# A two-branch mixer on one core: 64x64 fold tiles, more identity transposes, w1 loaded in whole rows, and three tiles' work ahead of the q fold

## The chip, the cores and the metric

The kernel runs on one NeuronCore of a Trainium2 chip. The metric is the time of one execution on the device in microseconds; before the change it was 660.29 us, the median of three runs (658.58 to 660.71). Five engines work side by side, each through its own list of instructions in order: PE (matrix multiplication, with its weight loads shown as PEld), DVE (vectors), ACT (activations), POOL and SP. SP and POOL, and ACT for one kind, also issue transfers (DMA).

## The reference

x is 2048 x 512. It is normalised, and then two branches are added to it: a linear attention with 32 heads of 16, whose feature map is a learned 16 x 16 matrix per head and two softmaxes, and a gated MLP whose gate mixes the rows.

```python
xn = _layernorm(x, axis=-1)
return x + _A_ref(xn, A_wqkv, A_w_phi, A_wo) + _B_ref(xn, B_w_in, B_w_sp, B_b_sp, B_w_out)
...
pq = jnp.einsum("bhsd,hdf->bhsf", q, w_phi)
pk = jnp.einsum("bhsd,hdf->bhsf", k, w_phi)
phi_k = jnp.concatenate([_softmax(pk, axis=-1), _softmax(-pk, axis=-1)], axis=-1)
kv = jnp.einsum("bhsf,bhsd->bhfd", phi_k, v)
z = jnp.einsum("bhsf->bhf", phi_k)
...
z = _gelu(jnp.einsum("bsd,df->bsf", x, w_in))
z2 = _layernorm(z[..., Fh:], axis=-1)
g = jnp.einsum("ts,bsf->btf", w_sp, z2) + b_sp[None, :, None]
return jnp.einsum("bsf,fd->bsd", z1 * g, w_out)
```

## The kernel before

x is taken in 16 tiles of 128 rows. To keep the precision of float32 with faster matmuls, every operand is held as two parts: h, the value rounded by ACT (`round_h`), and l, the rest, which DVE subtracts (`rest_l`). A product is then three matmuls, h by h, h by l and l by h (`mm3`, L49 to L53), so every product leaves rows with L51, L52 and L53.

The first phase, which this change touches, makes for each tile s: the centred x, its transpose xT by four PE transposes (L261), v (`proj_v`, 12 matmuls of 512 columns), k and q with their features (`proj_k`, `proj_q`; `softmax_pair` has DVE find maximum and minimum, subtract, ACT take the exponential, DVE sum and invert), the sum kv of k's features by v (`add_kv`, tile kvps, L291), and the first half z1 of the MLP's projection (`z1_raw`, tile zps, 24 matmuls of 344 columns), which ACT copies out of PSUM and sends to memory. Later phases make z2, the row mix (tile g, 30% of the chain of work that ended last) and the output; they are not touched.

The weights of q and k are not used as they come. The matrices of the heads are first multiplied into them: `fold(i, ...)` does it for k (i = 1) and q (i = 0) from the transposed weights wrow and the block-diagonal matrix bd. It is 128 small float32 matmuls, each of which leaves two PE and two PEld records in the trace; each contracts over 64 rows, writes 32 partitions and streams 64 columns, so that eight fit side by side in the array. `folded` then splits the four PSUM tiles into h and l: four ACT roundings and four DVE differences.

The order at the beginning is written by hand. `queue` is a stack of orders: each instruction given to `keep` must be issued, on its engine, before everything that is recorded later, until `queue.close()`. Behind that, a scheduler orders each engine's list. `warm_up(12)` puts 12 transposes of the identity on PE ahead of the first real work. Before the loop over tiles stand: tile 0 and 1 transposed, v(0), the k fold, v(1), k(0) with the transposes of tile 2 in its middle, the q fold. In the loop, tile s does k(s), then centres and transposes tile s + 2, then kv(s), v(s + 2) and its share of z1.

SP issues the loads in order: x of tiles 0 and 1, the four parts of wv, bd, the k weights, x of tile 2, the q weights, x of tile 3, the bias. w1, the weights of z1, comes in the loop at s = 1, in eight pieces of 128 x 344, through the five x slots (`load_win` with tag "x"), so these loads wait for x slots to be given back and later x tiles wait for them. Each piece is split by ACT and DVE on its own.

PSUM has eight banks. Those of za are taken in turn by the first half of a fold and by z1.

Of the kernel before, what the change touches and what calls it, by code (L numbers as in the profile page):

```python
# [10 lines left out]
F32 = mybir.dt.float32  # L11
# [18 lines left out]
XB = 5  # L30
# [5 lines left out]
def mixer(ctx: ExitStack, tc: tile.TileContext, x, x_t, wv, wqkT, phi_bd, wo, w_in, wst, b_r, w_out, out):  # L36
# [4 lines left out]
    def round_h(eng, h, src):  # L41
        if eng is act:
            return act.activation(h, src, AF.Copy).ins  # L43
        return eng.tensor_copy(h, src).ins
# [4 lines left out]
    def mm3(dst, a, b, start, stop):  # L49
        (ah, al), (bh, bl) = a, b  # L50
        pe.matmul(dst, ah, bh, start=start, stop=False)  # L51
        pe.matmul(dst, ah, bl, start=False, stop=False)  # L52
        return pe.matmul(dst, al, bh, start=False, stop=stop).ins  # L53
# [27 lines left out]
    def rstd_of(mv, r, stats=None):  # L81
        if stats is not None:
            dve.bn_aggr(mv, stats)
        pool.tensor_scalar_add(mv[:, 1:2], mv[:, 1:2], EPS_LN)
        pool.tensor_tensor(r, mv[:, 1:2], mhalf, op=ALU.pow)
# [11 lines left out]
    def bc(ap, n):  # L97
        return ap.unsqueeze(2).to_broadcast([P, n, DH])

    def softmax_pair(pl, src, tag, scale=1.0, ebufs=2):  # L100

        mm = pl.tile([P, 2, H], F32, tag=tag + "mm", bufs=1, name="mm")
        dve.tensor_reduce(mm[:, 0], heads(src), axis=AX.X, op=ALU.max)
        dve.tensor_reduce(mm[:, 1], heads(src), axis=AX.X, op=ALU.min)
        er = pl.tile([P, NF + 2 * H], F32, tag=tag + "e", bufs=ebufs, name="e")
        e, r = er[:, :NF], er[:, NF:]
        e2 = e.rearrange("p (h a d) -> p h a d", a=2, d=DH)
        dve.tensor_tensor(e2[:, :, 0], heads(src), bc(mm[:, 0], H), op=ALU.subtract)
        dve.tensor_tensor(e2[:, :, 1], bc(mm[:, 1], H), heads(src), op=ALU.subtract)  # L109
        act.activation(e, e, AF.Exp, scale=scale)  # L110
        sm = pl.tile([P, 2 * H], F32, tag=tag + "sm", bufs=1, name="sm")
        dve.tensor_reduce(sm, heads(e), axis=AX.X, op=ALU.add)  # L112
        dve.reciprocal(r, sm)
        return er
# [7 lines left out]
    def zproj(ps, s, w, order=(0, 1)):  # L122

        if ps in (za, kv_ps_p):
            p = [ps.tile([P, D], F32, tag="z", name="zps") for _ in range(2)]
        else:
            q = ps.tile([P, 2, D], F32, tag="z", name="zps")
            p = [q[:, k] for k in range(2)]
        t = xT[s]
        for k, j in enumerate(order):  # L130
            for c in range(ND):
                cs = slice(c * P, (c + 1) * P)
                mm3(p[k][:, :FC], (t[:, 0, cs], t[:, 1, cs]), (w[j][0][:, c], w[j][1][:, c]), c == 0, c == ND - 1)
        return [(slice(k, k + 1), p[k][:, :FC].unsqueeze(1)) for k in range(2)] if ps in (za, kv_ps_p) else [(slice(0, 2), q[:, :, :FC])]

    def z1_raw(pl, ps, s, bufs):
# [24 lines left out]
    with ExitStack() as p0:  # L161
# [13 lines left out]
        def stage(name, dt=F32):  # L175
            return xz.tile([P, 2, FH], dt, tag="xz", name=name)
# [15 lines left out]
        def fold(i, wT, tiles):  # L192


            for g in range(NG):
                for c in range(ND):
                    for m in range(4):
                        for r in range(2):
                            rows, cols = slice(r * HP, (r + 1) * HP), slice(m * QP, (m + 1) * QP)
                            ins = pe.matmul(tiles[c // 2][r][cols, c % 2, g], wT[g][rows, c * P + m * QP:c * P + (m + 1) * QP],  # L200
                                            bd[rows, g * P + r * HP:g * P + (r + 1) * HP], start=True, stop=True,
                                            skip_group_check=True).ins
            return ins

        def folded(i, tiles, keep=lambda **ins: None, between=lambda: None):
            for k in range(2):
                if k:
                    between()
                for r in range(2):
                    h, l = (w[:, i, 2 * k:2 * k + 2].rearrange("p c (g a b) -> p c g a b", g=NG, a=2)[:, :, :, r] for w in (wqk_h, wqk_l))  # L210
                    keep(act=round_h(act, h, tiles[k][r]))
                    keep(dve=rest_l(l, tiles[k][r], h))

        def fold_tiles(pools):
            return [[pl.tile([P, D], F32, tag=tag, name="fold").rearrange("p (c g b) -> p c g b", c=2, g=NG)
                     for _ in range(2)] for pl, tag in pools]
# [3 lines left out]
        def load_win(dst, j, stp, tag, bufs):  # L220
            for c in range(ND):
                t = stp.tile([P, D if tag == "x" else FC], F32, tag=tag, bufs=bufs, name="wst_")
                split_w(dst[0][:, c], dst[1][:, c], w_in[c * P:(c + 1) * P, j * FC:(j + 1) * FC], t[:, :FC])
# [10 lines left out]
        def fetch(s):  # L234
            if s < NT:
                xt[s] = load_x(s)

        def split_x(src):
            t = xz.tile([P, 2, FH], F32R, tag="xz", name="xT")
            xT.append(t)  # L240
            src = src.rearrange("p a b -> p (a b)")
            return round_h(act, t[:, 0, :D], src), rest_l(t[:, 1, :D], src, t[:, 0, :D])

        def stats(s, keep=lambda **ins: None):
            st6 = wk.tile([P, 6], F32, tag="st6", name="st6")
            dve.bn_stats(st6, xt[s])
            keep(dve=dve.bn_aggr(mv_x[:, s], st6).ins)

        def neg_mean(s):
            nm = wk.tile([P, 1], F32, tag="nm", name="nm")  # L250
            pool.tensor_scalar_mul(nm, mv_x[:, s, 0:1], -1.0)
            return nm

        def center(s, nm):
            return act.activation(xt[s], xt[s], AF.Identity, bias=nm).ins
# [13 lines left out]
            split_x(transposed(s)[0])  # L269

        def keep_v(s, p):
            v[s] = wk.tile([P, D], F32, tag="v", name="v")
            act.activation(v[s], p, AF.Copy, scale=r_x[:, s:s + 1])

        def proj_v(s):
            keep_v(s, proj(s, wv_h, wv_l))

        def proj_k(s):
            return softmax_pair(wk, proj(s, wqk_h[:, 1], wqk_l[:, 1]), "k", r_x[:, s:s + 1])
# [19 lines left out]
        fetch(2)  # L299
        wqT = load_rows(wqkT[:D])  # L300
        fetch(3)
        sp.dma_start(bias, b_r)


        def keep(**ins):
            for i in ins.values():
                queue.enter_context(tc.issue_after(i))

        def warm_up(n):

            t = ps.tile([P, ND, P], F32, tag="mm", name="idle")
            for k in range(n):
                i = pe.transpose(t[:, k % ND], ident, ident).ins
            keep(pe=i)
# [1 line left out]
        queue = ExitStack()  # L316
        tbl = wk.tile([P, 1], F32, tag="nm", name="tbl")
        keep(act=act.activation(tbl, mhalf, AF.Identity, bias=mhalf).ins)
        warm_up(12)
        stats(0, keep)  # L320
        keep(dve=dve.tensor_scalar(xt[0], xt[0], mv_x[:, 0, 0:1], None, op0=ALU.subtract).ins)
        stats(1, keep)
# [8 lines left out]
        def turned(s):  # L331
            pt, i = transposed(s)
            keep(pe=i)
            return pt

        def split_t(pt):
            i, j = split_x(pt)
            keep(act=i, dve=j)

        split_v(0)  # L340
        split_t(turned(0))
        for c in range(1, ND):
            split_v(c)
        keep(act=center(1, nm))
# [12 lines left out]
        keep(pe=fold(1, wkT, tiles))  # L357
        proj(1, wv_h, wv_l, p, (1, 2, 3))
        keep(pe=proj.last)
        stats(2, keep)  # L360
        nm = neg_mean(2)
        rstd_of(mv_x[:, 2], r_x[:, 2:3])
        folded(1, tiles, keep, lambda: keep(act=center(2, nm)))
        keep_v(1, p)
        kvps = kv_ps_p.tile([P, D], F32, tag="z", name="kvps")
        kv_acc = kvps[:, :NG * HP].rearrange("p (g b) -> p g b", b=HP)
        p = ps.tile([P, D], F32, tag="mm", name="proj")
        proj(0, wqk_h[:, 1], wqk_l[:, 1], p, (0, 1))
        keep(pe=proj.last)
        pt = turned(2)  # L370
        proj(0, wqk_h[:, 1], wqk_l[:, 1], p, (2, 3))
        keep(pe=proj.last)
        split_x(pt)
        ek = softmax_pair(wk, p, "k", r_x[:, 0:1])
        tiles = fold_tiles(((za, "z"), (ps, "mm")))
        keep(pe=fold(0, wqT, tiles))
        folded(0, tiles, keep)
        n1 = nq = 0
        for s in range(NT):
            fetch(s + 4)  # L380
            er = proj_k(s) if s else ek
            if 0 < s < NT - 2:
                centered(s + 2)
            while nq < (s - 2) * NT // (NT - 3):
                proj_q(nq)
                nq += 1
            add_kv(s, er)
            if s + 2 < NT:
                proj_v(s + 2)
            if s == 1:  # L390
                for j in range(2):
                    load_win(w1[j], j, wk, "x", XB)
                queue.close()
            while n1 < s * (NT - LAG) // (NT - 1):
                z1_raw(wk, za, n1, 2)
                n1 += 1

# [510 lines left out]
```

## Time and profile before

| | before |
|---|---|
| median of three runs | 660.29 us |
| the profiled execution, its own time | 660.35 us |
| its span, first to last instruction | 658.6 us |
| PE idle from 0 to 50 us, by its rows, beyond the 1.81 us at the start | 0.49, 0.69, 3.10, 1.72, 1.17, 2.46 us and smaller ones |
| PE idle from 50.2 to 215 us | none |

The profile page gives the busy time of each engine, and the span in 40 slices of 16.5 us, where a digit is a busy share in tenths. A row of the timeline gives start, length, engine, source line, operation, output and inputs, shape and count, and in brackets the idle time before it with what ended it. "issue" there means that the engine waited for nothing that the profile shows. A view by stages gives the busy time of every engine in each stretch and PEclk, the share of the full clock that was granted to PE.

### The profile page before, as it was taken

The page shows a single profiled execution, that of the slowest core. Times are in us where ns is not written, and L with a number is a line of the kernel's source. Part 1 is how long each engine was busy: PE and PEld are TensorE (multiplying, and loading weights), DVE is VectorE, ACT ScalarE, POOL GpSimd, SP SyncE. Part 2 cuts the span into 40 slices and gives each one's busy share as a digit, 9 for nine tenths or more (in the row PEclk, how much of TensorE's full clock was granted, in tenths as well). Part 3 has the DMA queues.
Part 4 walks back from the last instruction along what each step waited for, and adds up shares of the span by engine and source line. Part 5 has one row for each costly group of instructions (what it writes and reads, how often), then busy time and mean ns, then how long its engine had stood idle before and what let it go on. Part 6 is the DMA issues. An engine that isn't in the chain of part 4 may idle for free.

```text
span 658.6 us, 12104 instructions
## 1 busy us (share of the span) xinstructions
PE 642.5 (98%) x4740; PEld 577.6 (88%) x4740; DVE 509.4 (77%) x922; ACT 278.6 (42%) x463; POOL 97.0 (15%) x184
## 2 busy tenths in 40 slices
PE   7779999999999999999999999999999999999997
PEld 5658888888888999999999999999999878888885
DVE  4478798898889767999998687786787688989521
ACT  4344344343333264888544344344344332333330
POOL 4024122111101102554000100101000000000100
PEclk9789999999999999999999999999999999999999
DMA  8045436434434683000444534424448686775620
GB/s 313 15 98 142 129 104 172 131 88 133 129 102 135 191 286 124 32 1 25 133 131 133 169 113 137 161 89 169 126 146 273 199 316 245 284 252 218 237 66 32
DMA packets 39082, 98.45 MB, mean 149 GB/s; under 512 B 4881, under 2 KB 6929, under 8 KB 39025
## 3 DMA queue, kind: packets, MB, share of 16 engines
q1 hardware_dynamic: 27824, 56.78, 26.8%
q0 software_dynamic: 8896, 35.26, 17.7%
q10 hardware_dynamic: 2304, 5.64, 2.2%
q8 instruction: 37, 0.61, 0.4%
q14 instruction: 21, 0.16, 0.1%
HBM read 56.37 MB, written 26.61 MB: 126 GB/s over the span
## 4 chain that ended last, share of the span: by engine, by line
PE 94%; DMA 2%; DVE 2%; issue 1%; ACT 1%; SPq 0%; ACTq 0%
PE g L53 10%; PE g L51 10%; PE g L52 10%; PE proj L51 7%; PE proj L52 7%; PE proj L53 7%; PE zps L53 6%; PE zps L52 6%; PE zps L51 6%; PE pout L51 5%; PE pout L52 5%; PE pout L53 5%; PE po L803 1%; PE ptq L788 1%; PE kvps L291 1%; PE pout L817 1%
## 5 line engine op out<-in xcount | busy, mean ns | idle before, releaser
L51 PE MATMUL g<-B,A 128*128 128x344 f32 x448 | 143.3, 320 | 0.0
L53 PE MATMUL g<-B,A 128*128 128x344 f32 x448 | 143.3, 320 | 0.0
L52 PE MATMUL g<-B,A 128*128 128x344 f32 x448 | 143.2, 320 | 0.0
L53 PEld LDWEIGHTS g<-B,A 128*128 128x128 f32 x448 | 84.2, 188 | 0.0
L51 PEld LDWEIGHTS g<-B,A 128*128 128x128 f32 x448 | 84.2, 188 | 0.0
L52 PEld LDWEIGHTS g<-B,A 128*128 128x128 f32 x448 | 84.1, 188 | 0.0
L47 DVE TENSOR_TENSOR A<-S,A 128x512 fp32r<-128x512 f32 x64 | 43.7, 688 | 33.7 <-ACT A L43 32.9
L43 ACT ACTIVATE A<-S 128x512 fp32r<-128x512 f32 x64 | 40.0, 631 | 60.7 <-PE g L53 36.4
L110 ACT ACTIVATE e<-e,r_x 128x1024 f32<-128x1024 f32 x32 | 36.8, 1151 | 39.7 <-DVE e L109 39.2
L51 PE MATMUL proj<-wqk_h,xT 128*128 128x512 f32 x128 | 52.0, 407 | 0.0
L52 PE MATMUL proj<-wqk_l,xT 128*128 128x512 f32 x128 | 51.0, 399 | 0.0
L53 PE MATMUL proj<-wqk_h,xT 128*128 128x512 f32 x128 | 50.9, 398 | 0.0
L43 ACT ACTIVATE A<-wf 128x512 fp32r<-128x512 f32 x64 | 33.4, 522 | 36.9 <-PE g L53 33.1
L51 PE MATMUL zps<-w_0h,xT 128*128 128x344 f32 x128 | 41.6, 325 | 2.5 <-ACT w_0h L43 2.5
L112 DVE TENSOR_REDUCE sm<-e 128x64 f32<-128x1024 f32 x32 | 38.7, 1209 | 5.1 <-ACT e L110 5.0
L52 PE MATMUL zps<-w_0l,xT 128*128 128x344 f32 x128 | 41.3, 323 | 0.1
L53 PE MATMUL zps<-w_0h,xT 128*128 128x344 f32 x128 | 41.3, 322 | 0.0
L51 PE MATMUL zps<-w_1h,xT 128*128 128x344 f32 x128 | 41.2, 322 | 0.0
L53 PE MATMUL zps<-w_1h,xT 128*128 128x344 f32 x128 | 40.9, 320 | 0.0
L52 PE MATMUL zps<-w_1l,xT 128*128 128x344 f32 x128 | 40.8, 319 | 0.0
L47 DVE TENSOR_TENSOR A<-wf,A 128x512 fp32r<-128x512 f32 x64 | 35.4, 554 | 3.7 <-ACT A L43 3.3
L139 ACT ACTIVATE z1f<-zps,r_x 128x344 f32<-128x344 f32 (+1 forms) x29 | 16.4, 576 | 37.6 <-PE zps L53 32.6
(194 smaller groups left out, 1433.7 us busy)
## 6 DMA issues: line engine op xcount, KB each, us to landing
wf<-in_wst SPq DMA_DIRECT2D x64, 256.0 KB, 3.3
e_d<-e POOLq DMA_DIRECT2D x16, 544.0 KB, 4.6
et<-e_d SPq DMA_DIRECT2D x16, 544.0 KB, 5.5
zacc<-e POOLq DMA_DIRECT2D x16, 512.0 KB, 4.6
er<-et POOLq DMA_DIRECT2D x12, 512.0 KB, 4.0
u_d<-z1t POOLq DMA_DIRECT2D x16, 368.0 KB, 4.5
u<-u_d SPq DMA_DIRECT2D x15, 368.0 KB, 4.4
z_d<-z1f ACTq DMA_DIRECT2D x16, 344.0 KB, 3.6
```

The costliest lines, as they stand in the source:

```text
L43: return act.activation(h, src, AF.Copy).ins
L47: return (eng or dve).tensor_tensor(l, src, h.bitcast(F32), op=ALU.subtract).ins
L51: pe.matmul(dst, ah, bh, start=start, stop=False)
L52: pe.matmul(dst, ah, bl, start=False, stop=False)
L53: return pe.matmul(dst, al, bh, start=False, stop=stop).ins
L110: act.activation(e, e, AF.Exp, scale=scale)
L112: dve.tensor_reduce(sm, heads(e), axis=AX.X, op=ALU.add)
L139: act.activation(z[:, k], p, AF.Copy, scale=r_x[:, s:s + 1])
L291: pe.matmul(kv_acc[k:k + QP, m // 4], vs[:, m * QP:(m + 1) * QP], e[:, m * HP:(m + 1) * HP], start=s == 0 and m < 4, stop=s == NT - 1, ski ...
L788: pe.transpose(pt[:, a, k].bitcast(F32R), src, ident_r)
L803: lasts[3] = pe.matmul(po[r][c * QP:(c + 1) * QP, k], kvT[rows, m // 2, cols], fs[m // 4][rows, m // 2 % 2], start=True, stop=True).ins
L817: pe.matmul(p, rt, w, start=False, stop=False)
```

## The change

The fold takes 64 columns of weights at a time in place of 32: 64 matmuls, four side by side. `warm_up` makes 15 transposes of the identity in place of 12, and five more between the transposes of tile 0 and the first v. w1 is loaded in four whole rows of 128 x 688 behind x of tile 3, into slots that later hold xT, and is split by `split_w1` in four pieces of 128 x 688 in the middle of the softmax of k(0). Tile 3 is centred and transposed ahead of the loop. v(2), k(1) and z1(0) are issued ahead of the q fold, which moves into the loop's first pass. `v` gets a third buffer, and `queue.close()` moves from s = 1 to s = 3.

```diff
-    def softmax_pair(pl, src, tag, scale=1.0, ebufs=2):
+    def softmax_pair(pl, src, tag, scale=1.0, ebufs=2, meanwhile=lambda: None):
...
         act.activation(e, e, AF.Exp, scale=scale)
+        meanwhile()
         sm = pl.tile([P, 2 * H], F32, tag=tag + "sm", bufs=1, name="sm")
...
-                    for m in range(4):
+                    for m in range(2):
                         for r in range(2):
-                            rows, cols = slice(r * HP, (r + 1) * HP), slice(m * QP, (m + 1) * QP)
-                            ins = pe.matmul(tiles[c // 2][r][cols, c % 2, g], wT[g][rows, c * P + m * QP:c * P + (m + 1) * QP],
+                            rows, cols = slice(r * HP, (r + 1) * HP), slice(m * HP, (m + 1) * HP)
+                            ins = pe.matmul(tiles[c // 2][r][cols, c % 2, g], wT[g][rows, c * P + m * HP:c * P + (m + 1) * HP],
                                             bd[rows, g * P + r * HP:g * P + (r + 1) * HP], start=True, stop=True,
...
-            v[s] = wk.tile([P, D], F32, tag="v", name="v")
+            v[s] = wk.tile([P, D], F32, tag="v", bufs=3, name="v")
...
         fetch(3)
+        w1r = [stage("w1row") for _ in range(2)]
+        for c in range(ND):
+            sp.dma_start(w1r[c // 2][:, c % 2], w_in[c * P:(c + 1) * P, :FH])
         sp.dma_start(bias, b_r)
...
-        warm_up(12)
+        warm_up(15)
...
-        split_t(turned(0))
+        pt = turned(0)
+        warm_up(5)
+        split_t(pt)
...
+        keep(act=center(3, settled(3)))
         p = ps.tile([P, D], F32, tag="mm", name="proj")
         proj(0, wqk_h[:, 1], wqk_l[:, 1], p, (0, 1))
...
-        split_x(pt)
-        ek = softmax_pair(wk, p, "k", r_x[:, 0:1])
-        tiles = fold_tiles(((za, "z"), (ps, "mm")))
-        keep(pe=fold(0, wqT, tiles))
-        folded(0, tiles, keep)
-        n1 = nq = 0
+        split_t(pt)
+
+        def split_w1():
+            for j in range(2):
+                for k in range(2):
+                    h, l = (w[:, 2 * k:2 * k + 2] for w in w1[j])
+                    src = w1r[k][:, :, j * FC:(j + 1) * FC]
+                    keep(act=round_h(act, h, src))
+                    keep(dve=rest_l(l, src, h))
+
+        ek = [softmax_pair(wk, p, "k", r_x[:, 0:1], meanwhile=split_w1)]
+        proj_v(2)
+        keep(pe=proj.last)
+        ek.append(proj_k(1))
+        keep(pe=proj.last)
+        split_x(turned(3))
+        z1_raw(wk, za, 0, 2)
+        keep(pe=zproj.last)
+        n1, nq = 1, 0
         for s in range(NT):
             fetch(s + 4)
-            er = proj_k(s) if s else ek
-            if 0 < s < NT - 2:
+            er = ek[s] if s < len(ek) else proj_k(s)
+            if 1 < s < NT - 2:
                 centered(s + 2)
...
             add_kv(s, er)
-            if s + 2 < NT:
+            if s == 0:
+                tiles = fold_tiles(((za, "z"), (ps, "mm")))
+                keep(pe=fold(0, wqT, tiles))
+                folded(0, tiles)
+            elif s + 2 < NT:
                 proj_v(s + 2)
-            if s == 1:
-                for j in range(2):
-                    load_win(w1[j], j, wk, "x", XB)
-                queue.close()
...
+            if s == 3:
+                queue.close()
```

PE at its beginning, before, up to the first matmuls of v(0) (idle is the identity, pt the transposes of tile 0):

```order
L313 MATMUL idle<-ident 128x128 x12
L261 MATMUL pt<-ident,xt 128x128 x4
L51 MATMUL proj<-wv_h,xT 128x512
L52 MATMUL proj<-wv_l,xT 128x512
L53 MATMUL proj<-wv_h,xT 128x512
```

And after:

```order
L317 MATMUL idle<-ident 128x128 x15
L262 MATMUL pt<-ident,xt 128x128 x4
L317 MATMUL idle<-ident 128x128 x5
L51 MATMUL proj<-wv_h,xT 128x512
L52 MATMUL proj<-wv_l,xT 128x512
L53 MATMUL proj<-wv_h,xT 128x512
```

Eight transposes of the identity are added, three ahead of tile 0's and five behind them.

PE around the q fold, before: the end of k(0), the fold and the beginning of v(2).

```order
L51 MATMUL proj<-wqk_h,xT 128x512
L52 MATMUL proj<-wqk_l,xT 128x512
L53 MATMUL proj<-wqk_h,xT 128x512
L200 MATMUL fold<-bd,wrow 32x64 x128
L51 MATMUL proj<-wv_h,xT 128x512
L52 MATMUL proj<-wv_l,xT 128x512
```

After: the end of k(1), the transposes of tile 3, the ends of z1(0) and the fold with the beginning of v(3); v(2) and all of k(1) stand ahead of this piece.

```order
L52 MATMUL proj<-wqk_l,xT 128x512
L53 MATMUL proj<-wqk_h,xT 128x512
L262 MATMUL pt<-ident,xt 128x128 x4
L51 MATMUL zps<-w_0h,xT 128x344
...
L53 MATMUL zps<-w_1h,xT 128x344
L201 MATMUL fold<-bd,wrow 64x64 x64
L51 MATMUL proj<-wv_h,xT 128x512
L52 MATMUL proj<-wv_l,xT 128x512
```

The fold has half the instructions and has moved behind v(2), k(1), the transposes of tile 3 and z1(0).

ACT from the first two parts of the k fold on, before (the activations are the centring of tile 2, v(1), the rounding of xT(2) and the exponential of k(0)):

```order
L43 ACTIVATE wqk_h<-fold 128x8x64 x2
L255 ACTIVATE xt<-xt,nm 128x512
L43 ACTIVATE wqk_h<-fold 128x8x64 x2
L273 ACTIVATE v<-proj,r_x 128x512
L43 ACTIVATE xT<-pt 128x512
L110 ACTIVATE e<-e,r_x 128x1024
```

And after:

```order
L43 ACTIVATE wqk_h<-fold 128x8x64 x2
L256 ACTIVATE xt<-xt,nm 128x512
L43 ACTIVATE wqk_h<-fold 128x8x64 x2
L256 ACTIVATE xt<-xt,nm 128x512
L274 ACTIVATE v<-proj,r_x 128x512
L43 ACTIVATE xT<-pt 128x512
L43 ACTIVATE w_0h<-w1row 128x688 x2
L43 ACTIVATE w_1h<-w1row 128x688 x2
L274 ACTIVATE v<-proj,r_x 128x512
L110 ACTIVATE e<-e,r_x 128x1024
```

A second centring, that of tile 3, now stands ahead of v(1) and xT(2), and the four roundings of w1 and v(2) ahead of the exponential of k(0).

More of the change, by code (lines that the diff above doesn't have):

```diff
@@ L132, in zproj @@
                 cs = slice(c * P, (c + 1) * P)
-                mm3(p[k][:, :FC], (t[:, 0, cs], t[:, 1, cs]), (w[j][0][:, c], w[j][1][:, c]), c == 0, c == ND - 1)
+                zproj.last = mm3(p[k][:, :FC], (t[:, 0, cs], t[:, 1, cs]), (w[j][0][:, c], w[j][1][:, c]), c == 0, c == ND - 1)
         return [(slice(k, k + 1), p[k][:, :FC].unsqueeze(1)) for k in range(2)] if ps in (za, kv_ps_p) else [(slice(0, 2), q[:, :, :FC])]
@@ L359, in mixer, with settled @@
         keep(pe=proj.last)
-        stats(2, keep)
-        nm = neg_mean(2)
-        rstd_of(mv_x[:, 2], r_x[:, 2:3])
+        def settled(s):
+            stats(s, keep)
+            nm = neg_mean(s)
+            rstd_of(mv_x[:, s], r_x[:, s:s + 1])
+            return nm
+        nm = settled(2)
         folded(1, tiles, keep, lambda: keep(act=center(2, nm)))
```

## The prediction

> **What bounds the kernel now.** I read the page first, for the engine that is never free.
>
> ```profile
> PE 642.5 (98%) x4740; PEld 577.6 (88%) x4740; DVE 509.4 (77%) x922; ACT 278.6 (42%) x463; POOL 97.0 (15%) x184
> PE   7779999999999999999999999999999999999997
> PEclk9789999999999999999999999999999999999999
> q8 instruction: 37, 0.61, 0.4%
> ```
>
> PE is the bound: 98% busy, and below nine tenths only in the first three slices (49 us) and the last. So the change, which leaves PE's matrix work as it is, can gain only in those first slices, and everything it gains there must still stand when the full stretch begins. Next I cut that head into stages (columns: stage, its length, busy us of PE, PEld, DVE, ACT, POOL, granted clock, DMA share, GB/s).
>
> ```profile
> 18.44:27.30 8.86, 8.86 (x93) 6.94 (x93) 3.23 (x5) 3.95 (x7) 0.00 (x0) 0.67 0.03 8
> 27.30:29.12 1.82, 1.82 (x163) 1.65 (x163) 1.74 (x4) 0.00 (x0) 0.00 (x0) 1.00 0.23 76
> 30.84:44.80 13.96, 10.20 (x165) 8.15 (x165) 10.71 (x20) 6.17 (x13) 3.94 (x10) 1.00 0.37 78
> 44.80:48.20 3.40, 3.08 (x9) 2.15 (x8) 2.76 (x5) 3.40 (x7) 0.00 (x0) 0.50 0.39 113
> 48.20:69.08 20.88, 20.88 (x164) 17.73 (x164) 15.71 (x30) 9.53 (x15) 7.00 (x14) 1.00 0.60 155
> 69.08:215.00 145.92, 145.92 (x1029) 122.18 (x1028) 129.17 (x189) 54.13 (x68) 24.64 (x44) 1.00 0.44 123
> ```
>
> From 48.20 us PE has no idle time at full clock. Before that it loses time to idleness (3.76 us in 30.84 to 44.80) and to a halved clock (0.50 in 44.80 to 48.20, a mean of 0.67 in 18.44 to 27.30). PE's order in time shows the single losses (start, length, form, count, in brackets idle time and its releaser), and where to measure: 69.08, where v of tile 5 begins.
>
> ```profile
> 1.81 2.82 PE L313 MATMUL idle<-ident 128*128 128x128 f32 x12 [1.81 <-POOL ident masks.py:199]
> 5.12 1.11 PE L261 MATMUL pt<-ident,xt 128*128 128x128 f32 x4 [0.49 <-DVE xt L321]
> 6.92 0.79 PE L51 MATMUL proj<-wv_h,xT 128*128 128x512 f32 x1 [0.69 <-ACT xT L43]
> ...
> 13.27 2.07 PE L200 MATMUL fold<-bd,wrow 64*32 64x64 f32 x188
> 18.44 1.32 PE L200 MATMUL fold<-bd,wrow 64*32 64x64 f32 x68 [3.10 <-issue]
> ...
> 27.31 1.81 PE L200 MATMUL fold<-bd,wrow 64*32 64x64 f32 x162
> 30.84 1.17 PE L200 MATMUL fold<-bd,wrow 64*32 64x64 f32 x94 [1.72 <-issue]
> ...
> 39.66 0.66 PE L261 MATMUL pt<-ident,xt 128*128 128x128 f32 x4 [1.17 <-ACT xt L255]
> 43.57 0.42 PE L51 MATMUL zps<-w_0h,xT 128*128 128x344 f32 x1 [2.46 <-ACT w_0h L43]
> 69.08 0.40 PE L51 MATMUL proj<-wv_h,xT 128*128 128x512 f32 x1
> ```
>
> Each fold is broken by a stall named "issue": 3.10 and 1.72 us. Between the two stalls lie 93 + 163 = 256 PE and 256 PEld records, 512 instructions. The page has 37 packets on q8 for 4740 + 4740 records, about 256 a packet, and one packet fell into the first stall:
>
> ```profile
> q8 instruction: 1, 0.02, 2.1%
> ```
>
> (window 15.34 to 18.44). So I read the stalls as PE running out of code: the fold eats 256 records in about 3 us and the next block isn't there.
>
> The pitch of the matmuls comes from the chain (start, length, what):
>
> ```profile
> 10.28 0.43 PE proj L52
> 25.54 0.44 PE pt L261 x4
> 38.03 4.98 DMA wst__662<-in_w_in
> 54.83 0.31 PE zps L52 x2
> 60.58 0.23 PE proj L52
> 61.95 0.58 PE kvps L291 x32
> 62.53 0.43 PE proj L52
> ```
>
> A 512-wide projection costs 0.43 us at 10.28 and 0.23 at 60.58: the array runs at half speed early. zps costs 0.155, four transposes 0.44, a kvps group 0.58 plus 0.2 on the projection behind it. The 2.46 us wait is the w1 load, 4.98 us on the chain, whose issue had stood in SP's queue behind x slots.
>
> **The change, step by step.** I walk PE to the start of v of tile 5, the same set of work in both kernels (five v, five k, z1 of two tiles, six transposes, three kvps, both folds).
>
> ```profile
> 4.07 2.15 SPq L189 DMA_DIRECT2D wrow<-in_wqkT  x4
> 10.28 0.33 SPq L168 DMA_DIRECT2D xt<-in_x  x1
> DMA to landing us min/median/max: 3.5/5.4/5.9
> 6.90 2.00 ACT L43 ACTIVATE wv_h<-wrow 128x512 fp32r<-128x512 f32 x3
> 8.80 0.71 ACT L255 ACTIVATE xt<-xt,nm 128x512 f32<-128x512 f32 x1
> 20.91 1.08 ACT L43 ACTIVATE wqk_h<-fold 128x512 fp32r<-128x512 f32 x2
> 19.95 1.29 DVE L47 TENSOR_TENSOR wqk_l<-fold,wqk_h 128x512 fp32r<-128x512 f32 x2 [6.35 <-ACT wqk_h L43]
> 12.70 0.69 DVE L246 BATCH_NORM_STATS2 st<-xt 128x6 f32<-128x512 f32 x1
> 13.77 0.24 POOL L251 TENSOR_SCALAR nm<-mv_x 128x1 f32<-128x1 f32 x1 [6.11 <-DVE mv_x L247]
> 33.62 0.51 ACT L43 ACTIVATE w_0h<-wst__654 128x344 fp32r<-128x344 f32 x1
> 43.55 0.52 DVE L47 TENSOR_TENSOR w_0l<-wst__662,w_0h 128x344 fp32r<-128x344 f32 x1 [2.91 <-ACT w_0h L43]
> ```
>
> Identity transposes. 15 instead of 12 fill the 0.49 us ahead of pt(0), five more the 0.69 behind it, 5 x 2.82 / 12 = 1.2 us from about 6.0, so v(0) begins at 7.2 instead of 6.92. I take the array to be at full speed by then. Little follows directly: the wv parts are rounded until 8.90 and center(1) until 9.51, then pt(1) 0.44, xT(1) 0.6 + 0.7, and the last of the six v matmuls goes at about 11.6. Fold 1 starts at 11.8 instead of 13.27; its last operand, issued by 5.8, lands by 5.8 + 5.9 = 11.7. Gain 1.4.
>
> Fold in 64x64 tiles. 188 records in 2.07 us are 11 ns each with eight tiles side by side, 88 ns a tile; with four tiles 22 ns, and 128 records (64 matmuls, two each) take 2.8 us. Bounds: 11 ns (1.4 us), if the pace is per record, and 44 ns (5.6 us), if only two run together. I take 22, the row's own pace. Code: the first stall stands behind record 35 + 188 = 223 (12 idle, 4, 9, 4 and 6 matmuls ahead of the fold). Now fold 1 begins behind 43 records and ends at 43 + 128 = 171, and record 223 comes in k(1), at a pace of 0.23 us. Fold 2 holds records 249 to 376, and one block (128 records) past 223 lies in it; but 24 z1 matmuls, 3.7 us, lie between, more than the longer stall. Both stalls go. Fold 1 ends at 14.7 instead of 19.69: 5.0 ahead.
>
> Up to the end of k(0). v(1) 9 x 0.23 to 16.8; the wqk parts (ACT 0.54, DVE 0.65 each, center(2) between) are whole at 17.9; k(0) with pt(2) ends at 20.0. Before, at half clock, 27.31: 7.3 ahead.
>
> The new wait. ACT now has center(3) ahead of keep_v(1), xT(2) and the w1 roundings. x of tile 3 is there (10.28 + 5.4 = 15.7), but its statistics stand behind the four wqk differences on DVE: 17.9 + 0.9, POOL 0.5, so center(3) runs 19.3 to 20.0, keep_v(1) to 20.6, xT(2) to 21.2. v(2) behind it on PE waits 1.2 us, and 0.3 for the difference. Bounds 0 and 3.
>
> v(2), k(1), pt(3): 24 x 0.23 + 0.44 = 6.0, to 27.5. w1: a 344-wide rounding is 0.51, so a 688-wide one about 0.8; four end on ACT at 24.4, their differences, between the e operations on DVE, at 27.7, ahead of z1's second half at 29.4: hidden. If that cover went, z1 would wait as long as DVE is late. z1(0) ends at 31.3. The DMA queue of SP: 4 x 344 KB behind x(3) end near 19.4, and x(4), x(5) come behind them at about 21, with 6 us to spare.
>
> Fold 2 reuses the two banks of z1(0), so it waits for both ACT copies: 0.7 us, and ends at 34.9. Then 60 projections 13.8, 24 zps 3.7, two pt 0.9, three kvps 2.3: 20.7, to 55.6. kvps(0) needs its scaled e at 36.0 by the same count and comes at 38.4. I add 0.9 for hand-overs between engines, twice what PE is idle from 30.84 to 48.20 beyond the two named waits (4.08 - 1.17 - 2.46 = 0.45): 56.5.
>
> Sum: 69.08 - 56.5 = 12.6 us. By terms: fold 1 earlier 1.4; fold stalls and shares 3.6 + 1.8; half clock after fold 1 and after 44.80 about 2.1 + 1.5; idle for w1 and x, 1.17 + 2.46 and smaller ones, 4.4; new waits -2.2. Behind 69.08 the work is the same, PE has no idle time and DVE is busy 129.17 of 145.92, so I move the rest as it stands. The profiled execution took 660.35 us (658.6 of span, 1.75 around), next to the median 660.29: 660.35 - 12.6 = **647.8 us**.
>
> **Two rules of the skill.** The Trainium skill, "TensorE: Matmul & The Clock Gate", Part 4, says that transposes don't count as PE activity in the way that other matmuls do; by that the added transposes would not raise the clock. The trace agrees as far as it goes: nearly all work from 1.81 to 6.23 was transposes, and 10.28 still has 0.43. That is rival A.
>
> The Trainium skill, "Runtime: NRT & Kernel Launch", Instruction fetch mechanics, calls the cost of crossing a 256-instruction block mostly hidden, and gives PE room for 2048. By that the two stalls would not be code at all, and would stay. The spacing of 512 and the packet in the stall speak against it; it is rival B.
>
> **Rivals.**
> A, the transposes don't wake the array: v(0) runs at 0.43 to about 11, fold 1 starts at 13.2, 1.4 later. 649.2 us.
> B, the stalls belong to the fold's tile mode, so the change doesn't do what it says: 3.10 + 1.72 stay. 652.6 us, more if the clock falls again.
> C, the gain is spent behind: the waits of 1.5 and 0.7 us halve the clock (a stage of 3.4 us at 0.50 costs 1.7 each), or DVE, 89% busy in the loop, comes late to kvps each tile; 0.5 us in each of 14 tiles is 7. 651 to 660 us. Against it: DVE's list is no longer than before.
> D, slower: the folds' 64x64 tiles run one after another, 88 ns each: 128 x 88 = 11.3 us a fold, 8.5 more than counted, twice: 664.8 us. It decides from (2.8 + 6.3) x 1000 / 128 = 71 ns a record. For it: no row shows 64x64; against it: 11 ns a record shows eight tiles at once.
>
> **How the numbers follow.** Forecast 0.62, A 0.13, B 0.07, C 0.14 (0.09 of it still faster by over 0.3%, 0.05 within), D 0.04. 0.3%, about 2 us, is what a measurement of this kernel tells from no change. Faster 0.91, same 0.05, slower 0.04. Range: down 2.8 for folds at 11 ns and 1.5 for no wait, 643.5; up through A and B with both, 647.8 + 1.4 + 4.8 = 654. That leaves out D and most of C.
>
> **What would show it.** Fold rows of 64*64, 128 records without an "issue" gap, about 2.8 us each; clock 1.00 from about 7 us without a 0.50 stage; no wait on w1; ACT's center(3) near 19.3 released by POOL, and PE waiting for xT(2) just behind k(0); v(5) at 56.5. I am wrong if a fold keeps its gap or is over 5.6 us, if a half-clock stage stands behind 20 us, or if PE shows idle time between v(5) and 200 us.

## The result and the profile after

| | before | after |
|---|---|---|
| median, same chip | 659.94 us (658.58 to 660.71) | 649.34 us (647.49 to 650.03) |
| the profiled execution | 660.35 us | 648.69 us |
| its span | 658.6 us | 647.0 us |

The ratio is 0.9837 [0.9809, 0.9865]: 10.6 us faster by the medians, 1.5 us above the predicted 647.8. On two other chips, where the experiments ran, the same kernel gave 0.979 [0.9733, 0.9847] and 0.9778 [0.9746, 0.981].

From the page of the kernel after, the busy time of the engines, two rows of the 40 slices and the row of q8:

```profile
PE 637.1 (98%) x4492; PEld 573.8 (89%) x4492; DVE 508.7 (79%) x918; ACT 276.9 (43%) x459; POOL 98.2 (15%) x184
PE   8999999999999999999999999999999999999997
PEclk9999999999999999999999999999999999999999
q8 instruction: 35, 0.57, 0.4%
```

PE has 248 records fewer (the two folds lose 128 each, the added transposes give 8 back), and q8 two packets fewer. The digits 777 at the start have become 899, and the clock has no dip. The stages of the kernel after (stage, its length, busy us of PE, PEld, DVE, ACT, POOL, granted clock, DMA share, GB/s):

```profile
6.60:12.64 6.04, 5.43 (x23) 3.12 (x22) 4.05 (x7) 4.30 (x8) 0.55 (x1) 1.00 1.04 384
12.64:31.39 18.75, 17.86 (x206) 14.81 (x205) 14.26 (x24) 10.09 (x16) 2.24 (x7) 1.00 0.52 190
31.39:55.85 24.46, 23.38 (x317) 19.56 (x316) 22.63 (x39) 13.05 (x20) 9.46 (x20) 1.00 0.46 102
55.85:204.00 148.15, 148.15 (x1074) 123.91 (x1067) 128.93 (x190) 54.93 (x70) 25.67 (x44) 1.00 0.45 126
```

No stage has less than the full clock; PE's idle time between 12.64 and 55.85 us is 0.89 + 1.08 us, and none from there to 204. PE's order in time shows both folds whole and each of the two waits (start, length, form, count, in brackets the idle time ahead and its releaser):

```profile
6.03 0.96 PE L317 MATMUL idle<-ident 128*128 128x128 f32 x5
7.49 0.50 PE L51 MATMUL proj<-wv_h,xT 128*128 128x512 f32 x1 [0.51 <-ACT xT L43]
...
9.74 0.39 PE L52 MATMUL proj<-wv_l,xT 128*128 128x512 f32 x1
9.96 0.39 PE L53 MATMUL proj<-wv_h,xT 128*128 128x512 f32 x1
...
12.64 2.09 PE L201 MATMUL fold<-bd,wrow 64*64 64x64 f32 x128
...
21.13 0.50 PE L51 MATMUL proj<-wv_h,xT 128*128 128x512 f32 x1 [0.89 <-ACT xT L43]
...
31.39 2.49 PE L201 MATMUL fold<-bd,wrow 64*64 64x64 f32 x128
...
43.30 0.50 PE L51 MATMUL proj<-wv_h,xT 128*128 128x512 f32 x1 [1.08 <-ACT xT L43]
...
55.85 0.50 PE L51 MATMUL proj<-wv_h,xT 128*128 128x512 f32 x1
```

The last row is v of tile 5, which stood at 69.08 before: PE is 13.2 us ahead there, and 11.66 at the end (660.35 - 648.69). So everything was won in the first 56 us, and in this pair of executions 1.5 us of it were lost again later. The waits of PE from 55.85 us on, and one row of its weight loads, show where (in the first: who waited, for whom, us in total, times, longest):

```profile
PE ptu L703 <- DMA u<-u_d: 1.2, 1, 1.2
```

```profile
307.98 0.19 PEld L53 LDWEIGHTS g<-B,A 128*128 128x128 f32 x1 [0.43 <-DVE A L47]
```

The same view of before, from 69 us on, has one row:

```profile
PE ptu L677 <- DMA u<-u_d: 0.4, 1, 0.4
```

In the row mix (tile g) PE's weight load now waits 0.43 us for DVE, and behind it the load of u costs 1.2 us in place of 0.4. The tile ptu shows the lead on both sides of that load (line, tile, count: ns min/median/max, first and last start); before, and after:

```profile
L677 PE MATMUL ptu<-zb,u x60: 224/250/308, 517.3 to 632.9; 128*128 128x128 f32 x60
...
L677 PE MATMUL ptu<-zb,u_uh x4: 222/240/251, 508.0 to 508.2; 128*128 128x128 f32 x4
```

```profile
L703 PE MATMUL ptu<-zb,u x60: 223/249/304, 505.6 to 621.0; 128*128 128x128 f32 x60
...
L703 PE MATMUL ptu<-zb,u_uh x4: 224/238/252, 495.4 to 495.6; 128*128 128x128 f32 x4
```

508.0 - 495.4 = 12.6 us ahead of it, 517.3 - 505.6 = 11.7 behind it: in this pair PE came forward by more than the load did.

These are single executions, and the wait for u differs as much without any difference in lead. The first row is from the kernel before with the transposes alone, which is 0.4 us ahead there; the others are two executions of one kernel, the change with center(3) later (both are among the experiments):

```profile
PE ptu L679 <- DMA u<-u_d: 1.3, 1, 1.3
PE ptu L704 <- DMA u<-u_d: 0.2, 1, 0.2
PE ptu L704 <- DMA u<-u_d: 1.2, 1, 1.2
```

On the two other chips the medians of before and after lie 13.2 and 13.3 us apart (661.13 and 647.94, 660.79 and 647.53), as much as the lead at v(5) here. So that the lead itself costs the 1.5 us is not shown.

### The profile page after: what moved, and what is told of

Read it like the earlier page. It is cut to its first block, busy times and chain, and to the rows that moved or that the text cites. A ratio compares the mean times of both kernels' runs of the same rounds, so it can differ in the third digit from the quotient of the medians.

```text
span 647.0 us, 11586 instructions
## 1 busy us (share of the span) xinstructions
PE 637.1 (98%) x4492; PEld 573.8 (89%) x4492; DVE 508.7 (79%) x918; ACT 276.9 (43%) x459; POOL 98.2 (15%) x184
## 4 chain that ended last, share of the span: by engine, by line
PE 79%; DVE 6%; DMA 4%; issue 4%; POOL 4%; ACT 3%; SPq 0%; ACTq 0%; POOLq 0%; DVEq 0%
PE g L53 10%; PE g L51 10%; PE g L52 10%; PE proj L51 6%; PE proj L53 6%; PE proj L52 6%; PE pout L51 5%; PE pout L52 5%; PE pout L53 5%; PE zps L52 2%; PE zps L53 2%; PE zps L51 2%; PE po L829 1%; POOL rstd L85 1%; PE ptq L814 1%
## 5 line engine op out<-in xcount | busy, mean ns | idle before, releaser
L816 ACT ACTIVATE f<-ptq 128x512 f32<-128x512 f32 x32 | 16.5, 603 | 36.1 <-PE ptq L814 29.7
```

What stands on the lines that cost most here:

```text
L816: lasts[5] = act.activation(f, pt.rearrange("p a k b -> p a (k b)"), AF.Copy).ins
```

## The experiments

Two theories stood against each other. **Code:** the stalls in the folds come when PE has used up its instructions, so their place follows a count of records, and halving the fold's matmuls removes them. **Tile mode** (rival B): they belong to the fold's 32-column tiles. Beside that, what each further part of the change is worth, and whether the two waits that it brings matter.

| kernel | median us | ratio to before on the same chip |
|---|---|---|
| before + 64x64 fold | 655.56 | 0.9914 [0.9881, 0.9947] |
| before + transposes | 659.96 | 0.997 [0.9946, 0.9994] |
| before + both | 653.32 | 0.9863 [0.9828, 0.9898] |
| after, fold in 32 columns | 656.58 | 0.9913 [0.988, 0.9946] |
| after, each 64x64 matmul twice | 657.81 | 0.9947 [0.9926, 0.9968] |
| after, without the added transposes | 649.37 | 0.982 [0.9777, 0.9864] |
| after, center(3) later | 646.55, again 647.13 | 0.9775 [0.9732, 0.9818], 0.9773 [0.9742, 0.9804] |
| after, every early centring later | 645.94 | 0.9756 [0.9725, 0.9787] |
| after, run again beside these | 647.94, 647.53 | 0.979 [0.9733, 0.9847], 0.9778 [0.9746, 0.981] |

### The 64x64 fold alone

```diff
-                    for m in range(4):
+                    for m in range(2):
                         for r in range(2):
-                            rows, cols = slice(r * HP, (r + 1) * HP), slice(m * QP, (m + 1) * QP)
+                            rows, cols = slice(r * HP, (r + 1) * HP), slice(m * HP, (m + 1) * HP)
```

(and the slice of wT with HP in place of QP, as in the change)

> The kernel before with the 64x64 fold alone. If the fold's stalls are missing code, record 223 falls behind fold 1 and the later block ends fall outside both folds: no issue gap in a fold, about 2.1 to 2.5 us each, the half-clock stage behind fold 1 gone, the q fold over 6 to 7 us earlier than 31.94, and a total of 652 to 655 us. If the stalls belong to the tile mode or to the DMA traffic at that time, gaps of 3.1 and 1.7 us stay and the total is 658 to 660 us.

Measured: 0.9914, 5.7 us. PE's order in time shows both folds whole:

```profile
14.46 2.09 PE L200 MATMUL fold<-bd,wrow 64*64 64x64 f32 x128
21.99 2.09 PE L200 MATMUL fold<-bd,wrow 64*64 64x64 f32 x128
```

The gaps are gone without any of the other parts, and the median is a little above the 652 to 655 us expected. The count in the expectation has a slip: 35 + 128 + 25 = 188 records stand ahead of the second fold, so record 223 lies inside it, behind its 35th, and no gap stands there. So the end of a block alone doesn't stall PE; here 25 longer matmuls, from 16.48 to 21.99 us, stand between the two folds. The profiled execution was the longest of the nine (661.13 us, others 653.6 to 658.68), so only its rows up to the second fold are read here, and no total from it.

### The transposes alone

```diff
-        warm_up(12)
+        warm_up(15)
...
-        split_t(turned(0))
+        pt = turned(0)
+        warm_up(5)
+        split_t(pt)
```

> The kernel before with the eight added identity transposes alone. If they wake the array, v(0) runs at 0.23 us a matmul before 10 us, but the k fold still stalls, now behind its record 223 - 43 = 180, and the total is 658 to 660 us. If transposes do not count as activity, the pitch stays 0.43 to about 10.7 us and the total is 660 us.

Measured: 0.997, 2 us. The folds in PE's order in time:

```profile
12.13 1.99 PE L200 MATMUL fold<-bd,wrow 64*32 64x64 f32 x179
18.77 1.40 PE L200 MATMUL fold<-bd,wrow 64*32 64x64 f32 x77 [4.64 <-issue]
...
27.15 1.75 PE L200 MATMUL fold<-bd,wrow 64*32 64x64 f32 x154
30.66 1.25 PE L200 MATMUL fold<-bd,wrow 64*32 64x64 f32 x102 [1.76 <-issue]
```

Before, the stalls stood behind 188 and 162 fold records. Eight transposes more ahead of them, and they stand behind 179 and 154: nine and eight fewer, where eight were added. A stall that belonged to the tiles would have stayed at its matmul. Fold 1 started 1.1 us earlier than before (12.13 against 13.27), but the gap grew from 3.10 to 4.64 us, and the clock fell behind it:

```profile
16.70:23.50 6.80, 4.74 (x85) 3.88 (x85) 2.58 (x4) 2.67 (x5) 0.00 (x0) 0.50 0.03 7
```

So PE that came earlier waited longer: the stall ends nearly when it ended before (18.77 against 18.44).

### Both, without the w1 rows and the new order

The edit is the last two together.

> The kernel before with the 64x64 fold and the added transposes, without the w1 rows and the new order. My sum gives these two parts 1.4 + 3.6 + 1.8 + 2.1 = about 8 us of the gain, so 651 to 653 us, and the rest (about 3) to w1 and the order. If the head is bound by the w1 loads instead, the time saved in the folds is waited for again at z1(0): 656 us or more.

Measured: 0.9863, 9.0 us. What the w1 rows and the order still add is the step from here to the change: 1.7 us by 0.9837, 5.6 by 0.9778, so a few us, not better told, since the chips differ. The trace shows what it is made of. PE's order in time, and one stage of it:

```profile
28.68 0.65 PE L291 MATMUL kvps<-e,v 128*32 128x64 f32 x32 [1.14 <-DVE e L287]
...
30.29 0.61 PE L52 MATMUL zps<-w_0l,xT 128*128 128x344 f32 x1 [0.96 <-DVE w_0l L47]
...
35.66 0.65 PE L51 MATMUL zps<-w_0h,xT 128*128 128x344 f32 x1 [2.65 <-ACT w_0h L43]
```

```profile
30.40:40.60 10.20, 7.55 (x21) 5.69 (x22) 7.61 (x16) 5.61 (x10) 2.96 (x9) 0.50 0.64 144
```

With w1 in pieces behind the x slots, PE waits 0.96 and 2.65 us for it, and 1.14 for e; the clock is at half for 10.2 us. In the kernel after none of these rows is left.

### The change with the old fold

```diff
-                    for m in range(2):
+                    for m in range(4):
                         for r in range(2):
-                            rows, cols = slice(r * HP, (r + 1) * HP), slice(m * HP, (m + 1) * HP)
+                            rows, cols = slice(r * HP, (r + 1) * HP), slice(m * QP, (m + 1) * QP)
```

> The changed kernel with the 32-column fold back. Missing code: the stalls come back and stand where the count of records puts them, behind record 180 of fold 1 (223 - 43) and behind record 103 of fold 2 (479 - 376), a few more or less where records are missing; 654 to 657 us. Tile mode: stalls behind about the same records as before, 188 and 162. No stall at all: they came from the load traffic of before, and the total stays at 649 to 650 us.

Measured: 0.9913, so the rest of the change is worth 5.8 us without the fold. PE's order in time:

```profile
12.86 1.99 PE L201 MATMUL fold<-bd,wrow 64*32 64x64 f32 x179
19.39 1.16 PE L201 MATMUL fold<-bd,wrow 64*32 64x64 f32 x77 [4.54 <-issue]
...
37.06 2.72 PE L201 MATMUL fold<-bd,wrow 64*32 64x64 f32 x228
41.23 0.30 PE L292 MATMUL kvps<-e,v 128*32 128x64 f32 x2 [1.45 <-DVE e L288]
42.12 0.65 PE L292 MATMUL kvps<-e,v 128*32 128x64 f32 x30 [0.60 <-issue]
42.70 0.44 PE L201 MATMUL fold<-bd,wrow 64*32 64x64 f32 x28
```

Fold 1 breaks behind 179 records again. For fold 2 the expectation was a miss: no gap stands behind its record 103. The scheduler put the matmuls of kvps(0) into it behind record 228, where PE waits 1.45 us for DVE's e, and two records later PE stands still for 0.60 us named "issue". From the first gap to this one PE makes 77 records of fold 1, 77 of other work, 228 of fold 2 and 2 of kvps, 384 in all: three of the prediction's blocks of 128 records. And the gap stands at a matmul of kvps, not at one of the fold. It is one short gap, but it stands where the count puts it; against the tile mode it says nothing by itself, as kvps has tiles of 32 columns too.

### The 64x64 matmuls twice

```diff
-                    for m in range(2):
+                    for m in (0, 1, 0, 1):
```

The result is written twice with the same values; the count is that of the old fold, the tiles are those of the new.

> The changed kernel with each matmul of both folds issued twice, into the same place with the same operands, so 64x64 tiles and 256 records a fold. Missing code: fold 1 stalls again behind its record 179 or 180, as the 32-column fold with the same number of records did, for 3 to 4.6 us, and the q fold has a gap at a block end (records 103 or 231) if it has any; total 654 to 658 us. Tile mode: no issue gap, only twice the fold time, 2 x 2.1 to 2.5 us, 653 to 654 us at most.

Measured: 0.9947. PE's order in time:

```profile
12.20 2.89 PE L201 MATMUL fold<-bd,wrow 64*64 64x64 f32 x179
18.86 2.40 PE L201 MATMUL fold<-bd,wrow 64*64 64x64 f32 x77 [3.76 <-issue]
```

The same record, 179, with 64x64 tiles. This is what decides between the theories: tile form doesn't matter, the count does. Nor does the time since the fold began: the 179 records took 2.89 us here and 1.99 with the old fold. One packet of q8 falls into the gap, as before. Fold 2 is again mixed with kvps(0), and there it has no gap named "issue", at the places of the count (behind 102 and 230 records from its start) or elsewhere. So of the second stall only this is shown: it moved with the count in the run with the transposes alone, a short one stood at a place of the count in the run before this, and it is absent from every kernel with the halved fold. Which block ends stall PE and which don't is not shown beyond that.

### Without the added transposes

```diff
-        warm_up(15)
+        warm_up(12)
...
         pt = turned(0)
-        warm_up(5)
         split_t(pt)
```

> The changed kernel with 12 identity transposes and none behind tile 0's. If they buy what the run of before with them showed (about 2 us): half clock to 8 to 11 us in the records' pitch, fold 1 about 1 us later, 650 to 652 us. If the wv parts and their rounding bound v(0) anyway, no difference: 649 to 650 us.

> The changed kernel itself, on the same chip as the three above: 649 to 650 us, so that they are compared with it and not with the run on another chip.

Measured: 649.37 us (649.33 to 650.58) against 647.94 (646.6 to 649.4) for the change on the same chip. 1.4 us, which agrees with the 2 us of the run with the transposes alone, and is at the edge of what such runs tell. PE's order in time and two stages of the kernel without them:

```profile
7.22 0.50 PE L51 MATMUL proj<-wv_h,xT 128*128 128x512 f32 x1 [1.52 <-ACT xT L43]
...
13.82 2.10 PE L201 MATMUL fold<-bd,wrow 64*64 64x64 f32 x128
```

```profile
4.90:8.30 3.40, 1.63 (x7) 1.03 (x8) 2.46 (x6) 2.01 (x4) 1.77 (x5) 1.00 0.85 299
8.30:11.70 3.40, 3.40 (x11) 2.52 (x11) 1.63 (x3) 1.50 (x3) 0.00 (x0) 0.50 1.05 401
```

PE waits 1.52 us ahead of v(0), where five transposes would stand, is busy for 1.63 of 3.40 us, and the next 3.40 us go at half clock. Fold 1 begins at 13.82; with the transposes at 12.47 on the same chip:

```profile
12.47 2.09 PE L201 MATMUL fold<-bd,wrow 64*64 64x64 f32 x128
```

### The two new waits

The wait of 0.89 us at v(2) is ACT's: center(3) stands ahead of xT(2). First center(3) was moved behind it:

```diff
-        keep(act=center(3, settled(3)))
+        nm3 = settled(3)
...
         split_t(pt)
+        keep(act=center(3, nm3))
```

> The changed kernel with tile 3's centring behind keep_v(1) and the rounding of xT(2) on ACT. If the wait of PE at v(2) (0.89 us) is on the path: the wait is gone, v of tile 5 begins near 54.8 instead of 55.85 and the total is 648 to 649 us. If the lead is given back behind, as 1.3 us of it was in the changed kernel, v(5) begins earlier and the total stays within 0.3% of the changed kernel.

> e7 in more rounds: 646 to 647 us, 1 to 1.5 us below the changed kernel on the same chip; without a difference if the first comparison was chance.

Measured: 0.9775 and 0.9773. Beside the change on the same chip that is 646.55 against 647.94 us, and 647.13 against 647.53: 1.4 and 0.4 us, the second below the 1 to 1.5 expected, with ranges that overlap both times. So the two are not told apart by their times. In the trace the wait at v(2) went; the one at v(4) stayed (from the second run, PE's order in time):

```profile
42.11 0.50 PE L51 MATMUL proj<-wv_h,xT 128*128 128x512 f32 x1 [1.05 <-ACT xT L43]
```

ACT's rows in the kernel after show why: the centring of a later tile waits on ACT for POOL's nm, with xT(4), which v(4) needs, queued behind it.

```profile
41.46 0.72 ACT L256 ACTIVATE xt<-xt,nm 128x512 f32<-128x512 f32 x1 [2.60 <-POOL nm L252]
42.66 0.59 ACT L43 ACTIVATE xT<-pt 128x512 fp32r<-128x512 f32 x1
```

So each centring in the loop was tied behind the rounding of the tile ahead of it, too:

```diff
-            center(s, nm)
-            split_x(transposed(s)[0])
+            with tc.issue_after(rounded[-1]):
+                center(s, nm)
+            rounded.append(split_x(transposed(s)[0])[0])
...
-        split_x(turned(3))
+        rounded = [split_x(turned(3))[0]]
```

> The kernel e7 with each later tile's centring held on ACT behind the rounding of the tile before, so that none stands ahead of xT(4). If ACT's early centrings are what PE waits for at v(4) (1.05 to 1.12 us), that wait is gone as well, v of tile 5 begins 1 us earlier than in e7, and the total is 645 to 646 us. If the centring then comes too late for the transposes, PE waits for pt in the loop, each time by 0.5 us or more, and the total is 648 us or over. If the lead is trimmed behind, 646 to 647 us as e7.

> The changed kernel on the same chip, for the comparison with the two above: 647.5 to 650 us.

Measured: 645.94 us (644.52 to 647.59), the change beside it 647.53 (646.68 to 648.93). PE's order in time and its waits from 40 us to the end:

```profile
52.34 0.50 PE L51 MATMUL proj<-wv_h,xT 128*128 128x512 f32 x1
```

```profile
PE ptu L705 <- DMA u<-u_d: 1.0, 1, 1.0
PE g L51 <- ACT z L608: 0.4, 1, 0.4
PE g L53 <- DVE A L47: 0.3, 1, 0.3
```

v of tile 5 begins at 52.34, in the change beside it at 55.16, so 2.8 us earlier, with no wait on xT left. The waits at g and at u are the same 1.7 us in both, and the two profiled executions differ by 3.0 us (645.94 and 648.93): this lead was kept. But the one with 648.93 is the longest of its five runs, the medians differ by 1.6 us, and the ranges overlap. So it is the fastest of the kernels by its median, and that it beats the change is likely rather than shown.

## Why the prediction was right

By its own steps, forecast against the trace of the kernel after:

- **Forecast and rivals.** 647.8 against 649.34 us, faster, inside 643.5 to 654.0.
- **v(0) at 7.2, at full speed.** 7.49: ACT had to wait for the load of the first part of wv until 6.32 us (5.28 before), and rounded it ahead of xT(0). The speed was right: the projections from 9.74 to 9.96 are 0.22 apart, where before they stood 0.43 apart. Rival A falls. The Trainium skill, "TensorE: Matmul & The Clock Gate", Part 4, says that transposes don't count as PE activity in the usual way; the trace disagrees, since PE did nothing but transposes until 7.49 and ran fast from then on. (The profile lists them as MATMUL; whether they use the transpose mode that the section speaks of, it doesn't tell.)
- **Fold 1 from 11.8 to 14.7.** 12.64 to 14.7: it began 0.8 late, and took 2.09 us, not 2.8. The pace of a 64x64 record was mis-sized: 2.09 / 128 is 16 ns, between the 11 and the 22 that were weighed. D, at 71 ns a record, falls. The two errors cancel, so that the end came out at 14.7 is luck.
- **Both stalls go, because of code.** Right. That the place follows the count is shown for the first stall: 188 to 179 with the transposes, 179 with doubled 64x64 tiles. B falls. For the second the evidence is thinner: 162 to 154 with the transposes, and no DMA packet at all between 29.12 and 30.84 us before, so that it is missing code rests on the count. (Record 223 falls not in k(1) but in the transposes of tile 3 behind it, records 221 to 224 by the prediction's own count; nothing hangs on it.) The Trainium skill, "Runtime: NRT & Kernel Launch", Instruction fetch mechanics, calls a crossing of a block mostly hidden. The traces here agree where record 223 lies in the second fold of the kernel with the 64x64 fold alone, without a gap; in the bursts of 256 fold records they have gaps of 3.10, 1.72, 4.64, 4.54 and 3.76 us, and the measurement decides.
- **The new wait of 1.2 + 0.3 us at v(2).** 0.89, at 21.13 against 21.2. The mechanism was as told, center(3) at 19.29.
- **w1 hidden.** Right: no wait on w1 is left, and 0.96 + 2.65 us of them stand in the kernel with only the fold and the transposes.
- **Fold 2 from 32.0 to 34.9, behind a wait of 0.7 for ACT's copies.** Fold 2 began at 31.39, without the wait as idle time. The second copy ran beside the fold, which took 2.49 in place of 2.09; it ended 1.1 us early.

```profile
31.50 0.55 ACT L140 ACTIVATE z1f<-zps,r_x 128x344 f32<-128x344 f32 x1 [1.34 <-PE zps L53]
```

- **v(5) at 56.5.** 55.85. The 0.9 us added for hand-overs covered a wait that was not foreseen by place, the 1.08 at v(4).
- **"Behind 69.08 the work is the same ... so I move the rest as it stands."** This is the step that held least well. In the pair of profiled executions the lead of 13.2 us was 11.66 at the end. Between 55.85 and 204 us it holds (no idle time; rival C, DVE late at kvps in each tile, is not seen), and then 1.5 us go, 0.9 of them at the load of u and 0.43 at g. So C, a gain spent behind, may have come true in part, but neither by a fallen clock nor in the loop, the two places it named; and since the wait for u ran from 0.2 to 1.2 us in one kernel, the loss can as well be chance. Behind the start, 12.6 us was forecast and 13.2 found; at the end, 647.8 and 648.69. The 0.6 us more at the start and the 1.5 us less behind it have opposite signs, so part of the closeness at the end is luck.

## What to carry to other kernels

Count instructions where an engine issues many tiny ones: here PE stood still inside bursts of 256 matmul records, at a place that followed the count of instructions, as if it had outrun the delivery of its code, and the cure was half as many instructions with the same arithmetic, not a faster instruction. A stall of that kind moves with the count, so adding or doubling a few harmless instructions is a cheap way to tell it from a cause that belongs to one matmul or one moment. A lead that is won early may be trimmed at a later place where another engine or a transfer is nearly late, so look at the smallest margins there before carrying the whole of it to the end, and at more than one execution before calling a change of such a wait an effect.

## What the runs showed of the hardware that was not expected

- A 64x64 record costs 16 ns with four tiles side by side, a 64x32 record 11 ns with eight: half the instructions do the same fold in 2.09 us, against 1.81 + 1.17 in the second fold of before without its gap (in the first, 2.07 + 1.32, the last 68 records ran at half clock).
- PE that reaches the first code gap earlier waits longer: in four kernels the gap begins at 15.34, 15.10, 14.85 and 14.13 us and lasts 3.10, 3.76, 4.54 and 4.64, so all end between 18.44 and 19.39. What sets the end is not shown.
- 1.52 us of idle time, within 3.40 us that were 48% busy, was followed by 3.40 us at half clock; single waits of 0.89 and 1.08 us in the kernel after were not, nor was one of 1.33 us ahead of v(0) in the second run with center(3) later, with PE 61% busy from 4.90 to 8.30 us. Where the line lies is not shown.
